# Threshold attention and a token/channel MLP on one core: the second layer of the token MLP taken by halves of the tokens, its second half between later products

## The chip, the core and the metric

The kernel runs on one core of one Trainium2 chip. The metric is the device time of one execution in microseconds (us); five executions were timed and their median is the time given. All arithmetic is float32.

The core has five engines with a queue of instructions each: PE (TensorE, the matrix products, with its weight loads shown apart as PEld), DVE (VectorE), ACT (ScalarE), POOL (GpSimd) and SP (SyncE, which here only issues transfers). Each works through its queue in the order in which the program emitted it, and waits on semaphores for the others. Products are written to PSUM, from where DVE or ACT must take them.

## What is computed

```python
# q, k, v: (8, 8, 576, 64) = (row, head, token, dim)
scores = scale * q @ k.T                              # per row and head
thresh = max(scores, -1) - tau
scores = where(scores >= thresh, scores, -1e9)
attn = exp(scores - max(scores)) ; attn = attn / sum(attn)
x = (attn @ v) as (8, 576, 512)                       # token, model dim
# token MLP, mixes the tokens of a row
h = relu(x.T @ w_tok1) @ w_tok2                       # 576 -> 256 -> 576
u = x + h.T
# channel MLP, mixes the model dim of a token
out = u + relu(u @ w_ch1) @ w_ch2                     # 512 -> 1536 -> 512
```

## The kernel before

**Units.** The attention of the eight rows is cut into 144 units, 18 for each row (`units`, line 84). Row b holds units 18b to 18b+17, and a unit is 128 queries of two heads. The loop at line 614 emits for each unit u, in this order:

1. `scores(u)` (L304): the score products of both heads on PE, then two maxima on DVE (L309) and a bias on POOL (L310).
2. `norm(u-1)`: 1/sum on DVE (L333, L334) and the scaling on POOL (L337).
3. `fill(0.4)`: steps of MLP work, see below.
4. `turn_blocks(u-2)` (L367): a block transpose on DVE. After each third of them sixteen transfers `eT<-T` are issued on SP (L376), which complete the transpose of the attention weights.
5. `weigh(u)`: ACT's two threshold passes (L319), `fill(0.2)`, ACT's first exponential (L326), `fill(0.2)`, its second, `fill(0.2)`.
6. Loads of later q and k on ACT's queue, loads of v on SP's.
7. If a group of three units is due: `values` (L411, L416), the product with v on PE, which reads the tile that the sixteen transfers write. It is due two units after them. ACT copies its result into `xT` (L421).

When the last `values` of row b is done, `push(b)` (L579) puts the MLP work of the row on the queue of steps `todo`.

**The token MLP of a row** (`token_mlp`, L428) is 15 steps: five `turn_x` (L447, transposes on PE, copied by ACT, L448), two `tok1` (L454, ten matmul instructions, relu on ACT, L456), and eight `tok2(c, f)` (L464). `tok2(c, f)` makes, for the quarter c of the model dim and the half f of the tokens (288 each), two products (four matmul instructions) and adds them on DVE to `xT` (L468). The order before is c outside, f inside. For row 0 the first two quarters have been done earlier, at one step a unit (`early`).

**The channel MLP** (`channel_mlp`, L482) works on groups of 256 tokens of a pair of rows, five groups i = 0 to 4, the last of 128. The pair's even row pushes groups 0 and 1, the odd row groups 2, 3 and 4. So group 0 reads tokens 0 to 255 of the even row, and group 2 the last 64 of the even and the first 192 of the odd row. Each group is twelve `ch1(j)` (L507, eight matmul instructions, relu by ACT into `g`, L508), and for each of its two blocks of 128 tokens four `ch2(t, part)` of three products (L528, six matmul instructions of 512 columns). After the last part DVE adds u and writes `us` (L540; L546 in the first pair, where PE adds u by transposes, L524) and SP sends `us` to `out` (L547). From the second pair on, `ch1(1)` is followed by `turn_u` (L491), a DVE transpose of the group's u into the one buffer `us`, which therefore waits for the last `out` transfer of the group before; sixteen SP transfers (L497) then complete u in `ut`.

`tok1`, `tok2`, `ch1` and `ch2` share two PSUM buffers (`ps_mm`); a `ch2` block keeps one of them through all its parts. A product of the next step but one thus waits until DVE or ACT has emptied the buffer.

**The queue of steps.** Each step carries a cost. `push` takes what is left of the queue as `old`, puts one old step ahead of each token MLP step (two ahead of the steps in `waits`, the first `tok1` and the first `tok2`), then the rest of `old`, then the new groups. It sets `quota` = (sum of all costs - KEEP) / 17, KEEP being 45 (20 at row 0). `fill(share)` adds share x quota to the credit and emits steps as long as the credit is above zero, so the last one may overdraw it. Below, a unit's fills are called F.4, and the three F.2.

Of the kernel before, what the change touches and what calls it, by code (L numbers as in the profile page):

```python
# [21 lines left out]
def kernel(  # L22
# [36 lines left out]
    NP = H // 2  # L59
    NTK = DTOK // P  # L60
    NCC = DM // P
    NJ = DCH // P
# [162 lines left out]
    def weight(n):  # L225

        nonlocal steps_done
        for k in range(steps_done, min(steps_done + n, 3 * len(pieces) + 1)):
            i, part = divmod(k, 3)
            if part == 0:  # L230
                on_gpsimd(i - 1)
                if i:
                    load_piece(i - 1 + NRAW)
            else:
                on_scalar(i + 1, part - 1)
            on_vector(i, part)
            steps_done = k + 1
# [5 lines left out]
    def need(i):  # L243

        weight(3 * i + 4 - steps_done)
# [182 lines left out]
    def token_mlp(b, ps=range(NP)):  # L428

        xT = xTs[b]  # L430
        o = S * (b % 2)
        L = len(ps)
        cols = slice(P * ps[0], P * ps[0] + P * L)
        if b not in hidden:
            hidden[b] = work.tile([P, NTK, DM], F32, tag="a", bufs=1, name=f"a_{b}")
        a = hidden[b]

        def psum(name):
            return (ps_mm or ps_tr).tile([P, DM], F32, tag="mm" if ps_mm else "tr", name=name)

        def turn_x(t, n):
            M = MT[t]
            to = ps_tr.tile([P, MAIN], F32, tag="tr", name=f"tx_{b}_{t}_{ps[0]}")[0:M, 0 : n * L * P].rearrange("p (t c x) -> p t c x", t=n, c=L)
            for i in range(n):
                for c in range(L):
                    tok = o + (t + i) * P
                    nc.tensor.transpose(out=to[:, i, c, :], in_=xT[:, ps[c], tok : tok + M], identity=ident)  # L447
            nc.scalar.copy(out=x_sb[0:M, t : t + n, cols], in_=to.rearrange("q t p d -> q t (p d)"))  # L448

        def tok1(m):  # L450
            need(2)
            to = psum(f"t1_{b}_{m}_{ps[0]}")[:, 0 : P * L]
            for t in range(NT):
                nc.tensor.matmul(to, lhsT=w1[:, t, P * m : P * m + P], rhs=x_sb[:, t, cols], start=(t == 0), stop=(t == NT - 1))  # L454
            if ps_mm:
                nc.scalar.activation(out=a[:, m, cols], in_=to, func=AF.Relu)  # L456
            else:
                copies.append(lambda: nc.vector.tensor_scalar(out=a[:, m, cols], in0=to, scalar1=0.0, scalar2=None, op0=ALU.max))

        def tok2(c, f):  # L460
            need(6)
            to = psum(f"t2_{b}_{c}_{f}")[:, 0:HS]
            for m in range(NTK):
                nc.tensor.matmul(  # L464
                    to, lhsT=a[:, m, P * c : P * c + P], rhs=w2[:, m, HS * f : HS * f + HS], start=(m == 0), stop=(m == NTK - 1)
                )
            u = xT[:, c, o + HS * f : o + HS * f + HS]
            nc.vector.tensor_add(out=u, in0=u, in1=to)  # L468

        n = NI // L  # L470
        steps = [(0.11 * n * L, lambda t=t: turn_x(t, n)) for t in range(0, NI, n)] + [(0.11 * L, lambda: turn_x(NI, 1))]
        first = len(steps)
        steps += [(1.1 * L, lambda m=m: tok1(m)) for m in range(NTK)]
        steps += [(0.97, lambda c=c, f=f: tok2(c, f)) for c in ps for f in range(2)]
        return steps, (first, first + NTK)


# [4 lines left out]
    def channel_mlp(b, uT, i):  # L482

        s = {}
        n = min(GR, 2 * S - GR * i)
        nt = n // P

        def turn_u():

            us, ut = s["us"], s["ut"]  # L490
            nc.vector.transpose(  # L491
                out=us[:, 0:nt].rearrange("q n a (c d) -> q c (n a) d", c=NCC),
                in_=uT[:, :, GR * i : GR * i + n].rearrange("q c (m r) -> q c m r", r=32),
            )

            def move(a, k):
                nc.sync.dma_start(out=ut[32 * a : 32 * a + 32, 0:nt, k, :], in_=us[32 * k : 32 * k + 32, 0:nt, a, :])  # L497

            moves.extend([lambda a=a, k=k: move(a, k) for a in range(4) for k in range(4)])

        def ch1(j):
            need(7 + j)
            if j == 0:
                s["g"] = work.tile([P, NJ, GR], F32, tag="g", bufs=1, name=f"g_{b}_{i}")
            ps = ps_mm.tile([P, GR], F32, tag="mm", name=f"c1_{b}_{i}_{j}")[:, 0:n]
            for c in range(NCC):
                nc.tensor.matmul(ps, lhsT=wc1[:, j, c, :], rhs=uT[:, c, GR * i : GR * i + n], start=(c == 0), stop=(c == NCC - 1))  # L507
            nc.scalar.activation(out=s["g"][:, j, 0:n], in_=ps, func=AF.Relu)  # L508
            if j == 1:
                s["us"] = work.tile([P, GR // P, 4, NCC * 32], F32, tag="us", bufs=1, name=f"us_{b}_{i}")  # L510
                if b:
                    s["ut"] = work.tile([P, GR // P, 4, NCC * 32], F32, tag="ut", bufs=1, name=f"ut_{b}_{i}")
                    turn_u()

        def ch2(t, part):
            need(7 + NJ + 3 * part + 2)
            t0 = GR * i + P * t
            if part == 0:
                s["ps"] = ps_mm.tile([P, NCC, P], F32, tag="mm", name=f"c2_{b}_{i}_{t}")
            ps = s["ps"]  # L520
            flat = ps.rearrange("q c d -> q (c d)")
            if part == 0 and not b:
                for c in range(NCC):
                    nc.tensor.matmul(  # L524
                        ps[:, c, :], lhsT=uT[:, c, t0 : t0 + P], rhs=ident, is_transpose=True, start=(c == 0), stop=False, skip_group_check=True
                    )
            for j in range(3 * part, 3 * part + 3):
                nc.tensor.matmul(  # L528
                    flat,
                    lhsT=s["g"][:, j, P * t : P * t + P],  # L530
                    rhs=wc2[:, j, :],
                    start=(j == 0 and b > 0),
                    stop=(j == NJ - 1),
                    skip_group_check=True,
                )
            if part == 3:
                o = s["us"][:, t].rearrange("q a x -> q (a x)")
                if b:
                    move_u()
                    nc.vector.tensor_add(  # L540
                        out=o.rearrange("q (c k d) -> q c k d", c=NCC, k=4),
                        in0=ps.rearrange("q c (k d) -> q c k d", k=4),
                        in1=s["ut"][:, t].rearrange("q k (c d) -> q c k d", c=NCC),
                    )
                else:
                    nc.vector.tensor_copy(out=o, in_=flat)  # L546
                nc.sync.dma_start(out=out[b : b + 2].rearrange("b s d -> (b s) d")[t0 : t0 + P, :], in_=o)  # L547

        return [(0.0067 * n, lambda j=j: ch1(j)) for j in range(NJ)] + [
            (2.6 if part or b else 3.0, lambda t=t, part=part: ch2(t, part)) for t in range(nt) for part in range(4)  # L550
        ]

    def move_u():
        while moves:
            moves.popleft()()
# [6 lines left out]
    todo = deque()  # L562
# [16 lines left out]
    def push(b):  # L579
        nonlocal quota  # L580
        uT = xTs[b]
        steps, waits = token_mlp(b) if b else token_mlp(b, range(NP // 2, NP))
        old = list(todo)
        todo.clear()
        todo.extend(early)
        early.clear()

        for i, step in enumerate(steps):
            n = 2 if i in waits else 1
            todo.extend(old[:n] + [step])  # L590
            del old[:n]
        todo.extend(old)
        for i in range(2) if b % 2 == 0 else range(2, (2 * S + GR - 1) // GR):
            todo.extend(channel_mlp(b - b % 2, uT, i))
        quota = (sum(c for c, _ in todo) - (KEEP if b else KEEP_FIRST)) / (UB - 1)

    prep(0)
# [16 lines left out]
    for u in range(len(units) + LAG + 4):  # L614
# [4 lines left out]
        if on:  # L619
            b_now, p0, t = units[u]  # L620
            n = b_now * NP + p0
# [5 lines left out]
        last = False  # L627
        visit = False
        if due and not in_blocks(due[0][1]):
            visit = due[0][0] <= u  # L630
            last = values_due(u)
# [14 lines left out]
        if last and u < UB:  # L646
            early.extend(token_mlp(0, range(NP // 2))[0])
        elif last:
            push(0)
# [79 lines left out]
```

## Time and profile before

| | |
|---|---|
| median of 5 runs | 1354.51 us (1352.55 to 1356.74) |
| the profiled execution, device time | 1356.74 us |
| its span from first to last instruction | 1355.0 us |
| PE busy | 1307.7 us |
| DVE, ACT, POOL busy | 593.8, 585.2, 352.4 us |
| `tok2` matmuls (L464) | 256 instructions, 75.2 us; idle PE just ahead of them 8.1 us |
| `ch1` (L507), `ch2` (L528) matmuls | 401.4 us, 389.5 us |
| sixteen `eT<-T` transfers of a group, on SP's queue | 10.3 to 13.8 us to issue, median 2.3 us from issue to landing |

A line of the timeline gives the start in us, the length in us, the engine, the line of the kernel, the operation, output<-input, its shape and how many instructions are merged; in brackets the idle time of the engine before it and what ended it. In the list of groups the last columns are busy time, mean ns of one, and idle time before. PEclk is the granted clock of TensorE in tenths.

### The profile page before, as it was taken

The numbers are of one execution on the slowest core, as the hardware profiler recorded it, in microseconds if no ns is written. First come the engines' busy times: TensorE is split into PE (matmuls) and PEld (weight loads), VectorE is DVE, ScalarE is ACT, GpSimd is POOL, SyncE is SP. The second block draws the span as 40 slices with busy tenths as digits, with TensorE's granted clock in tenths as the row PEclk, the third lists the DMA queues.
The fourth block names the chain that finished last, engine by engine and source line by source line (L and its number), as shares of the span: only waits on it lengthen the run. The fifth ranks groups of instructions, "written<-read, shape, count | busy, mean of one in ns | idle before, by whom it ended". The sixth has DMA issues, their size and how long they took to land.

```text
span 1355.0 us, 17794 instructions
## 1 busy us (share of the span) xinstructions
PE 1307.7 (97%) x6138; PEld 810.5 (60%) x6138; DVE 593.8 (44%) x1024; ACT 585.2 (43%) x1299; POOL 352.4 (26%) x683
## 2 busy tenths in 40 slices
PE   6888899999999999999999999999999999999998
PEld 4555556547474666565665566465657566575675
DVE  6878884435443435434334444435443454201000
ACT  6876564444444435443434444344434454120110
POOL 4565652222322222212222222222221222100000
PEclk9998899999999999999999999999999999999999
DMA  5433764535354444543345434534443453400000
GB/s 122 119 94 112 203 157 106 127 93 132 88 133 91 110 107 100 125 110 87 87 105 128 97 85 117 129 81 110 113 101 83 114 117 78 113 22 17 23 24 32
DMA packets 296538, 135.31 MB, mean 100 GB/s; under 512 B 204736, under 2 KB 289216, under 8 KB 296448
## 3 DMA queue, kind: packets, MB, share of 16 engines
q1 hardware_dynamic: 167840, 118.15, 34.2%
q10 hardware_dynamic: 128608, 16.01, 7.4%
q8 instruction: 49, 0.80, 0.2%
q14 instruction: 41, 0.34, 0.1%
HBM read 43.25 MB, written 9.44 MB: 39 GB/s over the span
## 4 chain that ended last, share of the span: by engine, by line
PE 87%; DVE 5%; ACT 3%; DMA 2%; SPq 1%; issue 1%; POOL 1%; ACTq 0%; DVEq 0%; POOLq 0%
PE c L528 27%; PE c L507 27%; PE sc L304 11%; PE pv L416 8%; PE t L454 5%; PE t L464 4%; PE pv L411 3%; DVE mx L309 2%; ACT e L319 1%; PE tx L447 1%; SPq L376 1%; DMA lk<-in_k_dram 1%; PE tr L355 1%; ACT e L326 1%; DMA scratch<-in_moe_w_ch_dram 0%
## 5 line engine op out<-in xcount | busy, mean ns | idle before, releaser
L507 PE MATMUL c<-xT,wc 128*128 128x256 f32 (+1 forms) x1920 | 401.4, 363 | 0.1
L309 DVE TENSOR_REDUCE mx<-sc 128x1 f32<-128x576 f32 x288 | 204.3, 750 | 447.8 <-PE sc L304 447.7
L528 PE MATMUL c<-wc,g 128*128 128x512 f32 x864 | 389.5, 597 | 0.0
L507 PEld LDWEIGHTS c<-xT,wc 128*128 128x128 f32 x1920 | 335.6, 191 | 69.9 <-issue 29.7
L310 POOL TENSOR_SCALAR bias<-mx,toff 128x1 f32<-128x1 f32 x288 | 81.6, 283 | 781.0 <-DVE mx L309 724.2
L319 ACT ACTIVATE e<-sc,bias 128x576 f32<-128x576 f32 x288 | 199.4, 739 | 181.9 <-POOL bias L310 177.9
L528 PEld LDWEIGHTS c<-wc,g 128*128 128x128 f32 x864 | 158.9, 190 | 181.6 <-issue 177.9
L326 ACT ACTIVATE e<-e,ntau 128x576 f32<-128x576 f32 x288 | 221.0, 771 | 0.0
L337 POOL TENSOR_SCALAR e<-e,rr 128x576 f32<-128x576 f32 x288 | 214.4, 756 | 14.7 <-ACT g L508 2.6
L508 ACT ACTIVATE g<-c 128x256 f32<-128x256 f32 (+1 forms) x240 | 86.6, 361 | 297.6 <-PE c L507 279.4
L304 PE MATMUL sc<-kT,qT 64*128 64x288 f32 (+1 forms) x1280 | 194.2, 436 | 13.2 <-DVE kT L286 7.1
L367 DVE STREAM_TRANSPOSE T<-e 128x1152 f32<-128x1152 f32 x126 | 172.0, 1365 | 5.5 <-DMA eT<-T 3.3
L304 PEld LDWEIGHTS sc<-kT,qT 64*128 64x128 f32 (+1 forms) x1280 | 107.6, 180 | 99.9 <-issue 57.7
L416 PE MATMUL pv<-eT,lv 128*64 128x384 f32 (+1 forms) x1024 | 137.1, 408 | 0.0
L416 PEld LDWEIGHTS pv<-eT,lv 128*64 128x64 f32 x1024 | 76.3, 138 | 49.6 <-issue 41.4
L421 ACT COPY xT<-pv 128x384 f32<-128x384 f32 (+1 forms) x56 | 21.0, 400 | 165.6 <-PE pv L416 163.7
L540 DVE TENSOR_TENSOR us<-c,ut 128x512 f32<-128x512 f32 x27 | 18.6, 690 | 155.0 <-PE c L528 137.9
L464 PE MATMUL t<-w,a 128*128 128x288 f32 x256 | 75.2, 421 | 8.1 <-DVE xT L468 4.7
L454 PE MATMUL t<-x_sb,w 128*128 128x512 f32 (+1 forms) x180 | 73.4, 555 | 0.0
L464 PEld LDWEIGHTS t<-w,a 128*128 128x128 f32 x256 | 45.8, 192 | 30.2 <-issue 10.5
L468 DVE TENSOR_TENSOR xT<-xT,t 128x288 f32<-128x288 f32 x64 | 28.3, 446 | 71.0 <-PE t L464 70.5
L326 ACT ACTIVATION_READ_ACCUMULATOR e<-e,ntau 128x1 f32 x288 | 56.6, 197 | 0.0
(46 smaller groups left out, 542.6 us busy)
## 6 DMA issues: line engine op xcount, KB each, us to landing
eT<-T SPq DMA_DIRECT2D x672, 108.0 KB, 2.3
scratch<-in_moe_w_ch_dram SPq DMA_DIRECT2D x24, 512.0 KB, 3.7
lv<-in_v_dram SPq DMA_DIRECT2D x32, 288.0 KB, 3.4
out_dram<-us SPq DMA_DIRECT2D x36, 256.0 KB, 2.2
lk<-in_k_dram ACTq DMA_DIRECT2D x111, 72.0 KB, 2.7
lq<-in_q_dram ACTq DMA_DIRECT2D x106, 72.0 KB, 2.3
ut<-us SPq DMA_DIRECT2D x192, 32.0 KB, 1.9
lq<-in_q_dram SPq DMA_DIRECT2D x22, 72.0 KB, 3.2
```

Of the source, the lines that this page charges most:

```text
L304: nc.tensor.matmul(sc[h][rows, f, 0:HS], lhsT=qT[r, cols], rhs=kT[r, HS * f : HS * f + HS], start=True, stop=True)
L309: nc.vector.tensor_reduce(out=mx[:, c], in_=sc[h][:, :, 0:HS], axis=AX.XY, op=ALU.max)
L319: nc.scalar.activation(out=eh, in_=sc[h][:, :, 0:HS], func=AF.Prelu, bias=bias[:, h : h + 1], scale=SCALE, alpha=STEEP)
L326: nc.scalar.activation(out=eh, in_=eh, func=AF.Exp, bias=ntau, accum_out=rs[:, h : h + 1])
L337: nc.gpsimd.tensor_scalar(out=eh, in0=eh, scalar1=rr[:, h : h + 1], scalar2=1.0, op0=ALU.mult, op1=ALU.mult)
L367: nc.vector.transpose(out=T[:, :, place, :].rearrange("p a (c x) -> p c a x", c=NK), in_=e.rearrange("p (c a x) -> p c a x", c=NK, a=4))
L416: nc.tensor.matmul(to[r], lhsT=lv[:, j, :], rhs=e[j], start=False, stop=(c == NI - 1), skip_group_check=True)
L454: nc.tensor.matmul(to, lhsT=w1[:, t, P * m : P * m + P], rhs=x_sb[:, t, cols], start=(t == 0), stop=(t == NT - 1))
L464: nc.tensor.matmul(to, lhsT=a[:, m, P * c : P * c + P], rhs=w2[:, m, HS * f : HS * f + HS], start=(m == 0), stop=(m == NTK - 1))
L507: nc.tensor.matmul(ps, lhsT=wc1[:, j, c, :], rhs=uT[:, c, GR * i : GR * i + n], start=(c == 0), stop=(c == NCC - 1))
L508: nc.scalar.activation(out=s["g"][:, j, 0:n], in_=ps, func=AF.Relu)
L528: nc.tensor.matmul(flat, lhsT=s["g"][:, j, P * t : P * t + P], rhs=wc2[:, j, :], start=(j == 0 and b > 0), stop=(j == NJ - 1), skip_group_ ...
```

## The change

`tok2` now runs through all four quarters c for the first half of the tokens, then for the second half. `push` takes the second half (four steps, two for row 0) off the token MLP and puts them between the first `ch1` steps of the row's first new group: `ch1(0)`, `tok2`, `ch1(1)`, `tok2`, and so on. With eleven token steps instead of fifteen, fewer old steps are used up among them. At `waits` row 1 takes three old steps at both places, rows 2, 4 and 6 three ahead of the first `tok2`, the others two as before. In group 1 of the first pair (`b == 0 and i == 1`), which is the old work of row 1, a `ch2` step holds one product instead of three (J = 1).

```diff
-        steps += [(0.97, lambda c=c, f=f: tok2(c, f)) for c in ps for f in range(2)]
+        steps += [(0.97, lambda c=c, f=f: tok2(c, f)) for f in range(2) for c in ps]
...
+        J = 1 if b == 0 and i == 1 else 3
...
-        def ch2(t, part):
-            need(7 + NJ + 3 * part + 2)
+        def ch2(t, part, J):
+            need(7 + NJ + J * part + J - 1)
...
-            for j in range(3 * part, 3 * part + 3):
+            for j in range(J * part, J * part + J):
...
-            if part == 3:
+            if J * part + J == NJ:
...
-            (2.6 if part or b else 3.0, lambda t=t, part=part: ch2(t, part)) for t in range(nt) for part in range(4)
+            (0.867 * J + (0.0 if part or b else 0.4), lambda t=t, part=part: ch2(t, part, J)) for t in range(nt) for part in range(NJ // J)
...
         steps, waits = token_mlp(b) if b else token_mlp(b, range(NP // 2, NP))
+        half = NP if b else NP // 2
+        last = steps[-half:]
+        del steps[-half:]
...
         for i, step in enumerate(steps):
-            n = 2 if i in waits else 1
+            n = (3 if b == 1 or (b % 2 == 0 and i == waits[1]) else 2) if i in waits else 1
             todo.extend(old[:n] + [step])
             del old[:n]
         todo.extend(old)
+        new = []
         for i in range(2) if b % 2 == 0 else range(2, (2 * S + GR - 1) // GR):
-            todo.extend(channel_mlp(b - b % 2, uT, i))
+            new.extend(channel_mlp(b - b % 2, uT, i))
+        for i, step in enumerate(last):
+            new.insert(2 * i + 1, step)
+        todo.extend(new)
```

## The prediction, made before the changed kernel was run

> **What bounds the kernel now.** I read the page's busy times and slices first, then the list of groups, then PE's timeline from end to end for its gaps, and last SP's timeline beside it.
>
> ```profile
> PE 1307.7 (97%) x6138; PEld 810.5 (60%) x6138; DVE 593.8 (44%) x1024; ACT 585.2 (43%) x1299; POOL 352.4 (26%) x683
> ...
> PE   6888899999999999999999999999999999999998
> ...
> L464 PE MATMUL t<-w,a 128*128 128x288 f32 x256 | 75.2, 421 | 8.1 <-DVE xT L468 4.7
> ```
>
> PE sets the end. Its work isn't touched: the same instructions run, in another order. Only its gaps can change: 1355.0 - 1307.7 = 47.3 us, of which some 26 lie ahead of 133 us, where hardly anything is moved, and 3.9 at the very end. That leaves about 17. The groups put 8.1 of them ahead of tok2. One by one, in PE's timeline:
>
> ```profile
> 140.09 2.29 PE L464 MATMUL t<-w,a 128*128 128x288 f32 x4 [2.91 <-DVE xT L468]
> 161.82 1.87 PE L304 MATMUL sc<-kT,qT 64*128 64x288 f32 x8 [2.57 <-ACT e L319]
> 163.63 7.08 PE L507 MATMUL c<-xT,wc 128*128 128x256 f32 x24
> ...
> 250.33 0.55 PE L411 MATMUL pv<-eT,vl 128*64 128x192 f32 x4 [2.46 <-DMA lk<-in_k_dram]
> 285.79 0.63 PE L447 MATMUL tx<-ident,xT 128*64 128x128 f32 x4 [1.23 <-ACT x_sb L448]
> 304.31 1.24 PE L464 MATMUL t<-w,a 128*128 128x288 f32 x4 [1.26 <-DVE xT L468]
> 309.38 3.23 PE L464 MATMUL t<-w,a 128*128 128x288 f32 x12 [0.52 <-DVE xT L468]
> 433.16 0.87 PE L411 MATMUL pv<-eT,vl 128*64 128x384 f32 x4 [0.34 <-ACT e L326]
> 458.70 1.24 PE L464 MATMUL t<-w,a 128*128 128x288 f32 x4 [1.58 <-ACT g L508]
> 774.03 1.24 PE L464 MATMUL t<-w,a 128*128 128x288 f32 x4 [0.82 <-ACT g L508]
> 830.88 1.90 PE L304 MATMUL sc<-kT,qT 64*128 64x288 f32 x8 [0.78 <-ACT e L319]
> ```
>
> The waits for tok2 are short ones for a PSUM buffer. The second bound is less plain: the wait at 250.33 is named a load, but it ends 2.56 us after SP has issued the group's sixteen eT transfers (234.57 + 13.20 = 247.77). `values` waits for those, and in rows 1 and 2 they are hardly ever early. The same comparison two units on from 366.76, where unit 52 starts:
>
> ```profile
> 371.08 13.41 SPq L376 DMA_DIRECT2D eT<-T  x16
> ...
> 387.23 0.55 PE L411 MATMUL pv<-eT,vl 128*64 128x192 f32 x4
> ```
>
> Issue ends at 384.49, the last lands some 2.2 later (1.9 to 2.6 where PE waited for it) at 386.7, and PE arrives at 387.23: 0.5 us to spare. So the question is which steps stand between a group's sixteen transfers and its `values`.
>
> **How the order was worked out.** I carried costs, quota and credit through the units for both orders. Row 1, for instance: quota before (129.4 - 45)/17 = 4.97, after (130.3 - 45)/17 = 5.02, so a unit gets 1.99 in F.4 and 0.99 in each F.2. The order before agrees with the trace (unit 43 gets tok2 in each F.2: 300.85 x8, 304.31 x4). Durations used: scores 1.17 (start to next start), ch1 1.79 (x24 takes 5.38), a ch2 step of three 2.67, tok2 0.97 to 1.07.
>
> **Part 1, tok2 by halves.** Nothing is added on any engine or queue; 28 + 2 steps move later, behind 1 to 4 of the new ch1. ch1(0) now follows the adds of the first half more closely.
> - Row 0, unit 22. Before: tok2, tok2, [2.91], tok2, ch1(0). After: tok2, ch1(0), whose last quarter needs that add. The add sits on DVE behind the maxima of unit 22 as before (139.59), so PE has 1.5 us of ch1 to run from 136.05 and then waits 2.6. The wait at 161.82 follows a weight load that SP issues behind the sixteen transfers of this unit; with one add (0.45) less ahead of the transpose these start 0.4 earlier. **Gain 0.4** (bounds -1.0 and +2.9).
> - Row 1: the third tok2 of unit 43 still finds both buffers full (1.26 stays). In unit 44 ch1(0) waits some 0.3 for the last add instead of 0.52. **Gain 0.2.**
> - Row 2, unit 63: three small ch1 instead of two ahead of tok2. The third waits 0.9 for its buffer, tok2 0.3 more, but 0.98 of work more is done: 1.58 + 0.98 - 1.2 - 0.9. **Gain 0.5** (0 to 1.6). Rows 4 and 6: the third ch1 meets the same wait that tok2 met. **0.** In F.4 two tok2 with one small ch1 between them show a gap of 0.24 (782.87 starts 1.13 after 781.74 where 0.89 is usual); by the new order row 4 loses one such place and row 6 gets two. **Loss 0.3.**
> - Rows 3, 5, 7 show no gap before. After, the half moved stands between ch1 of 1.79, and each add ends some 3.5 us into its unit (maxima 1.42, norm 0.35, add 0.45 behind scores 1.17), PE needing the buffer at 4.0. **0**; without that cover it would be 0.4 a row.
>
> **Part 2, older work.** Before, 5.2 cost is left when row 1 is pushed, two steps; after, 6.07, seven single products (the first group's two boundaries fall otherwise). They go between the five turn_x, and the 0.24 and 1.23 idle ahead of them go: ACT needs 0.57 for each copy, a product covers 0.87. **Gain 1.3** of 1.47. None is left for the first tok1's third place, nor for tok2: the "three" of row 1 does nothing. A switch between products of two tiles shows up to 0.10 in the lengths (2.84 against 2.74), seven of them at most 0.7; I take 0, as most rows after a turn_x read 2.74.
>
> **Part 3, what the shift does to `values`.** In each window I compared work before and after, and when the transfers start. Most have over 1 us to spare. The tight ones:
> - Unit 36 (250.33): single products overdraw less, two instead of three ahead of it. **Loss 0.9**, the gap becomes 3.3.
> - Unit 54 (387.23): one ch2 step (the second of group 2's second block) slips from unit 52 into 51, and nothing comes in its place; 2.67 less in the window against 0.5 to spare. **Loss 2.2** (0.5 to 2.7). Unit 51 gets the 2.67, where there was no gap to fill.
> - Unit 60 (433.16): 2.67 more. **Gain 0.3.**
> - Units 69 and 105. The last ch2 of the old group, with its output, slips from behind the sixteen transfers to ahead of them (unit 67 and 103, F.4). The transpose now waits for that product and add: 1.17 + 2.6 + 0.69 against 3.05 after the unit's start, 1.5 later, and 0.35 for the out transfer on SP. `values` had 0.1 and 0.7 to spare, with +0.5 and -0.3 of work. The load on ACT's queue that lengthened the issue (13.80 and 12.41, against 10.30 undisturbed) is then partly past. **Loss 0.6 and 1.0** (0 to 2.0 each).
>
> The same slip ends a worse thing on DVE:
>
> ```profile
> 492.89 13.80 SPq L376 DMA_DIRECT2D eT<-T  x16
> 506.80 0.53 SPq L547 DMA_DIRECT2D out_dram<-us  x1
> ...
> 509.10 1.25 DVE L491 STREAM_TRANSPOSE us<-xT 128x1024 f32<-128x1024 f32 x1 [8.00 <-DMA out_dram<-us]
> 827.80 1.25 DVE L491 STREAM_TRANSPOSE us<-xT 128x1024 f32<-128x1024 f32 x1 [10.01 <-DMA out_dram<-us]
> ```
>
> turn_u held DVE for 8.00, 10.01 and (row 6) 3.31 us until the output behind the transfers had gone. PE paid only once, at 830.88: 0.78 idle and scores of 1.90 instead of 1.24. **Gain 1.4.**
>
> **Sum.** Gains 0.4 + 0.2 + 0.5 + 1.3 + 0.3 + 1.4 = 4.1; losses 0.3 + 0.9 + 2.2 + 1.6 = 5.0. Net +0.9. The profiled execution took 1356.74, 1.74 more than its span and 2.2 more than the median, so it would take 1357.6; the median goes from 1354.5 to **1355.4**.
>
> A rule is to be weighed here. The gap of 2.57 at 161.82 cost clock (twelve products in 7.08 instead of 5.45, scores 1.87 for 1.24; granted clock 0.63 from 164 to 168 us), the gap of 2.46 at 250.33 none (1.00). So from the rows alone a gap of 3.3 or 2.2 may cost nothing, or 0.63 + 1.63 + 0.62 = 2.9; I take 0, the nearest row in place. The Trainium skill (TensorE: Matmul & The Clock Gate, Part 1: The HAM clock gate) says the clock halves after an idle window of about 3.4 us that runs freely; the two rows show that 2.5 can already do it and need not. By the page a full cold window at unit 36 would cost some 1.7 us, an estimate, making the sum 1357.1.
>
> **Rivals.**
> 1. *Faster: the transfers keep up.* For it: landing times run from 2.2 to 4.3 us and issue from 10.3 to 13.8, and a shift of ACT's loads out of the issue alone would save 3 us at units 54, 69 and 105. Against: ACT's loads follow the units and still fall inside. Then the losses of 3.8 there (2.2 + 1.6) go: 1355.4 - 3.8 = 1351.6; if the tok2 waits go wholly as well (2.6 + 1.3 + 0.3 + 1.1 + 1.6 = 6.9) 1344.7. I put it at 1350.
> 2. *Slower: the longer gaps cool the clock*, at unit 36, at 54, or both: 1355.4 + 2.9 = 1358.3, or 1361.2. It decides from the point where a gap loses clock, which the rows only place near 2.5.
> 3. *Slower: turn_u blocks the moved adds.* The second tok2 of the half moved is behind turn_u on DVE. If the output still stands behind the sixteen transfers, DVE is held 8.0, 10.0 and 3.3 us; PE gets through tok2, ch1 and scores (4 us), then stands: 4 + 6 = 10 more, 1365. By the queue arithmetic the output comes in F.4, ahead of them; one step later and it doesn't.
> 4. *Part 2 doesn't do what it says*, if the single products all go ahead of the token steps: 1355.4 + 1.3 = 1356.7; no other sign than the forecast's.
>
> **How the numbers follow.** This kernel's measurement can tell about 0.2% (2.7 us) from no change: 1351.8 to 1357.2. Forecast with rival 4: 0.44, its own range 1351.8 to 1357.2 (its bounded terms add to about 2.5 either way). Rival 1: 0.26. Rival 2: 0.21. Rival 3: 0.09. Faster 0.26, the same 0.44, slower 0.30. The range reaches into rivals 1 and 2, to 1350.0 and 1360.5, leaving out the far end of rival 1 and rival 3.
>
> **What would show it.** PE's gaps: none ahead of turn_x near 285; 1.26 still ahead of a tok2 in unit 43; about 3.3 ahead of the `values` of unit 36, 2 ahead of that of unit 54, about 1 ahead of those of 69 and 105; L491 without its waits of 8 and 10, and no 0.78 near 831. Wrong would be a wait of DVE at L491 followed by one of PE at L464, a granted clock under 0.9 behind unit 36 or 54, or no gap at `values` of 54.

## The result, and the profile after

| | before | after |
|---|---|---|
| median | 1354.5 us (1350.66 to 1358.75, 51 runs) | 1357.53 us (1354.11 to 1362.27, 29 runs) |
| ratio to before, 95% interval | | 1.0025 [1.0019, 1.0031] |
| the profiled execution, and its span | 1356.74, 1355.0 us | 1360.33, 1358.5 us |

The changed kernel is 3.0 us slower, 2.1 us above the forecast, inside the range. 0.25% is just past what was called no change.

The page of the changed kernel: engines' busy time, the granted clock in 40 slices, and two groups of the list.

```profile
PE 1310.7 (96%) x6138; PEld 812.8 (60%) x6138; DVE 592.1 (44%) x1024; ACT 584.0 (43%) x1299; POOL 352.7 (26%) x683
...
PEclk9998999999999999999999999999999999999999
...
L464 PE MATMUL t<-w,a 128*128 128x288 f32 x256 | 76.3, 422 | 1.4 <-DVE xT L468 1.3
L411 PE MATMUL pv<-eT,vl 128*64 128x384 f32 (+1 forms) x256 | 46.7, 433 | 9.1 <-DMA lq<-in_q_dram 4.5
```

The change did to tok2 what it says: idle PE ahead of L464 falls from 8.1 to 1.4 us. Idle time ahead of `values` (L411) rises to 9.1 (5.2 in the list of before), and ahead of ch1 (L510) to 6.1 (0.1 at L507 before). PE's timeline, the gaps that matter:

```profile
142.06 1.22 PE L510 MATMUL c<-xT,wc 128*128 128x256 f32 x2 [2.59 <-DVE xT L468]
162.82 1.86 PE L304 MATMUL sc<-kT,qT 64*128 64x288 f32 x8 [1.58 <-ACT e L319]
...
250.60 0.65 PE L411 MATMUL pv<-eT,vl 128*64 128x192 f32 x4 [2.71 <-DMA lq<-in_q_dram]
305.25 1.24 PE L464 MATMUL t<-w,a 128*128 128x288 f32 x4 [1.26 <-DVE xT L468]
319.29 1.99 PE L510 MATMUL c<-xT,wc 128*128 128x256 f32 x8 [0.55 <-DVE xT L468]
390.07 0.55 PE L411 MATMUL pv<-eT,vl 128*64 128x192 f32 x4 [1.49 <-DMA eT<-T]
...
536.92 0.55 PE L411 MATMUL pv<-eT,vl 128*64 128x192 f32 x4 [1.25 <-DMA lk<-in_k_dram]
854.08 0.55 PE L411 MATMUL pv<-eT,vl 128*64 128x192 f32 x4 [1.26 <-DMA lq<-in_q_dram]
```

Nothing is left ahead of turn_x near 285, nor at 831. New are `values` of units 54 (390.07), 72 (536.92) and 108 (854.08), and a ch1 in unit 46 (319.29). The gap of unit 36 (250.60) is only 0.25 longer than before, but it now costs clock. The windows view has stretch, length, busy time of each engine (instructions), granted clock, DMA share and GB/s:

```profile
251.00:254.00 3.00, 3.00 (x22) 2.86 (x20) 0.00 (x0) 0.00 (x0) 0.00 (x0) 0.50 0.30 56
```

TensorE ran at half clock there. The same stretch of before, by its own gap of unit 36:

```profile
250.00:252.00 2.00, 1.67 (x21) 1.70 (x23) 0.00 (x0) 0.00 (x0) 0.00 (x0) 1.00 0.50 112
252.00:255.00 3.00, 3.00 (x32) 2.24 (x27) 0.00 (x0) 0.54 (x2) 0.00 (x0) 1.00 0.00 0
```

To add up what no single gap shows, I took for each matmul the time from its start to the next one's start, less the usual one for its kind and shape in before. This excess by stretch (us from the start), for before, after and runs that are told of below:

```
               before  after |    e1     e5     e6     e8     e9
 131 to 172     12.83  10.65 | 10.74   9.63  16.10  10.02  10.50
 172 to 230      3.54   4.61 |  5.82   4.06   3.02   4.95   8.45
 230 to 260      3.73   5.70 |  3.06   3.79   1.47   3.11   1.51
 260 to 300      3.45   1.50 |  3.41   4.80   1.51   3.03   1.48
 300 to 345      3.91   4.59 |  4.39   3.16   3.14   3.14   3.23
 380 to 415      1.69   2.83 |  1.59   1.47   1.40   3.03   1.39
 485 to 530      2.14   1.68 | 10.09   1.66   1.65   1.73   1.49
 530 to 580      1.88   3.02 |  1.82   1.83   2.61   1.73   1.83
 800 to 830      2.06   1.10 |  3.24   2.68   1.04   2.47   1.24
 830 to 885      2.66   3.58 |  2.00   2.02   2.05   2.05   2.05
1070 to 1120     3.17   4.38 |  3.90   3.43   3.69   3.83   3.68
all from 131    65.22  66.96 | 74.67  61.59  59.91  62.48  59.10
```

The sums move by some tenths of a us, up to 0.7 in a stretch, with what is taken as usual, so only the larger differences are read. In this pair of profiles the change is worth +1.7 us. The other 1.9 us of the two spans' difference of 3.5 lie ahead of 131 us, before anything is moved.

### The profile page after: what moved, and what is told of

Read it like the earlier page. It is cut to its first block, busy times and chain, and to the rows that moved or that the text cites. A ratio compares the mean times of both kernels' runs of the same rounds, so it can differ in the third digit from the quotient of the medians.

```text
span 1358.5 us, 17797 instructions
## 1 busy us (share of the span) xinstructions
PE 1310.7 (96%) x6138; PEld 812.8 (60%) x6138; DVE 592.1 (44%) x1024; ACT 584.0 (43%) x1299; POOL 352.7 (26%) x683
## 4 chain that ended last, share of the span: by engine, by line
PE 85%; DVE 6%; DMA 3%; ACT 2%; issue 1%; POOL 1%; SPq 0%; ACTq 0%; DVEq 0%; POOLq 0%
PE c L532 27%; PE c L510 25%; PE sc L304 11%; PE pv L416 9%; PE t L454 5%; PE t L464 4%; PE pv L411 3%; DVE mx L309 2%; DMA lq<-in_q_dram 1%; PE tx L447 1%; ACT e L319 1%; DMA lk<-in_k_dram 1%; PE tr L355 1%; DVE scratch L203 1%; ACT e L326 1%
## 5 line engine op out<-in xcount | busy, mean ns | idle before, releaser
L510 PE MATMUL c<-xT,wc 128*128 128x256 f32 (+1 forms) x1920 | 402.3, 361 | 6.1 <-DVE xT L468 3.3
L510 PEld LDWEIGHTS c<-xT,wc 128*128 128x128 f32 x1920 | 333.7, 190 | 73.8 <-issue 24.2
L464 PE MATMUL t<-w,a 128*128 128x288 f32 x256 | 76.3, 422 | 1.4 <-DVE xT L468 1.3
L464 PEld LDWEIGHTS t<-w,a 128*128 128x128 f32 x256 | 46.4, 192 | 22.2 <-issue 10.6
L411 PE MATMUL pv<-eT,vl 128*64 128x384 f32 (+1 forms) x256 | 46.7, 433 | 9.1 <-DMA lq<-in_q_dram 4.5
```

The source lines that it names most:

```text
L411: nc.tensor.matmul(to[r], lhsT=vl[:, r], rhs=e[NI], start=True, stop=False, skip_group_check=True)
L464: nc.tensor.matmul(to, lhsT=a[:, m, P * c : P * c + P], rhs=w2[:, m, HS * f : HS * f + HS], start=(m == 0), stop=(m == NTK - 1))
```

## The experiments

Ratios are to runs of before on the same chip in the same set; its medians there were 1356.08 (e1 to e4), 1353.66 (e5 to e8) and 1355.6 us (e9 to e12).

**e1, the halves alone.** After, but with ch2 steps of three products and two older steps at the waits everywhere:

```diff
-        J = 1 if b == 0 and i == 1 else 3
+        J = 3
...
-            n = (3 if b == 1 or (b % 2 == 0 and i == waits[1]) else 2) if i in waits else 1
+            n = 2 if i in waits else 1
```

> tok2 by halves and its second half between the ch1, but steps of three products in all groups and two older steps at both waits, as before. Theory (the single products are the loss: they leave 0.87 us of cost more or less in a unit, which moves a whole ch2 step over a unit's boundary in later rows): no gap of its own ahead of the values of units 36, 54 and 72, idle gaps there as in the kernel before (2.5, 0, 0 us); the wait of 8 us of DVE at turn_u in row 2 may stay, the gaps ahead of turn_x (1.6) stay; row 0 some 1 us better. Time 0 to 2 us below before. Rival (the halves are the loss: ch1 and tok2 wait for the adds, and the adds stand behind turn_u): 2 to 3 us above before, with gaps at tok2 and ch1.

1367.27 us, 1.0088 [1.0074, 1.0102], against all that was expected. The timeline shows one place; rows of SP, DVE and PE:

```profile
492.40 13.36 SPq L376 DMA_DIRECT2D eT<-T  x16
505.87 1.10 SPq L551 DMA_DIRECT2D out_dram<-us  x1
...
508.63 1.25 DVE L494 STREAM_TRANSPOSE us<-xT 128x1024 f32<-128x1024 f32 x1 [9.00 <-DMA out_dram<-us]
...
511.53 3.78 PE L510 MATMUL c<-xT,wc 128*128 128x256 f32 x8 [6.05 <-DVE xT L468]
```

The last output of the old group stands on SP behind the sixteen eT transfers. turn_u, which overwrites `us`, waits on DVE for it until 508.63. The moved tok2's add (L468) is queued behind turn_u and ends at 511.5, and the ch1 that needs the add's PSUM buffer leaves PE idle for 6.05 us. The granted clock is 0.56 from 509 to 513 us and 0.58 from 513 to 517. This is the third rival of the prediction, and it costs 8 us of excess (10.09 against about 2) in this one unit.

**e2, the single products alone.** Before with J = 1 in group 1 of the first pair; tok2 in its old order and place.

> Steps of a single product in the older work of row 1, nothing else: tok2 in the old order, all of it ahead of ch1, two older steps at both waits. Theory (the single products are the loss): the gaps ahead of turn_x are gone (1.6 to 1.9 us gained), and gaps appear ahead of the values of unit 54 (1.5 to 2.2 us) and unit 72 (1.4), the gap of unit 36 is 0.3 to 0.9 longer, with a window of half clock after it in some executions (1.7): 1.5 to 3 us above before. Rival (the halves are the loss): 1 to 2 us below before, since only the gaps at turn_x change.

1357.59 us, 1.0009 [0.9999, 1.002], between the two expectations and not clear of no change. The turn_x gaps go, as they should (excess of 260 to 300: 1.50), but `values` of unit 54 waits 1.31 and unit 36's gap of 2.43 is followed by half clock from 252.08 on. The gap foreseen at unit 72 isn't there. What one place gains, two others lose.

**e3 and e4, the third older step.** e3 is after with J = 3 (halves and threes), e4 is after with n = 2 at all waits (halves and singles).

> The change with steps of three products in all groups, the three older steps at the waits kept. Theory: like the run with the halves alone, within 1 us, so 0 to 2 us below before; row 1 has only two older steps for its fifteen places, so three or two makes nothing there, and in rows 2, 4 and 6 the wait of 0.8 to 1.7 us moves from tok2 to a ch1. Rival (the halves or the third older step are the loss): 2 to 3 us above before.

> The change with two older steps at both waits everywhere, single products and halves kept. Theory: as the changed kernel within 1 us, 2 to 4 us above before; the gaps at the values of units 36, 54 and 72 stay. Rival (the third older step is the loss): at or below before.

e3: 1366.8 us, 1.0083 [1.0069, 1.0096], with e1's stall: the threes don't remove it. e4: 1360.58 us, 1.0027 [1.0014, 1.004], like after (1.0025). The third older step is worth nothing that can be measured. So it is the single products that take the stall away from the halves: they leave 0.87 more cost in the queue, and the old group's last output slips ahead of the sixteen transfers. After's SP queue shows it, 1.3 us between the two:

```profile
496.47 0.36 SPq L551 DMA_DIRECT2D out_dram<-us  x1
497.80 10.96 SPq L376 DMA_DIRECT2D eT<-T  x16
508.87 14.13 SPq L500 DMA_DIRECT2D ut<-us  x16
523.12 10.95 SPq L376 DMA_DIRECT2D eT<-T  x16
```

The last two rows are the source of unit 72's gap: the sixteen ut transfers come right behind the eT transfers and take 14.13 us to issue; the next sixteen eT start at 523.12, though their block transposes were done at 520.2. In before the ut transfers start later, behind a pause of the queue, and take less time:

```profile
510.37 10.19 SPq L497 DMA_DIRECT2D ut<-us  x16
```

Two loads go out on ACT's queue during either set (512.73 and 513.09 after, 512.89 and 515.44 before); the last section comes back to that.

**e5, the stall's cause taken away.** e1, with turn_u issued at the eighth ch1 of a group instead of the second, when all moved adds are ahead of it:

```diff
-            if j == 1:
+            if j == 7:
                 s["us"] = work.tile(
```

> The halves of the tokens alone (steps of three and two older steps at the waits, as before), but the transpose turn_u is issued with the eighth ch1 of a group instead of the second, behind all moved tok2 steps. Theory (turn_u, which waits on VectorE for the out transfer behind sixteen eT transfers, holds up the moved adds; that alone makes the halves 11 us slower): the 6.05 us gap in unit 67 and the 6.8 us of half clock behind it go, the excess of 485 to 530 falls from 10.1 to about 2, and the time is 0.999 to 1.002 of before. Rival (the moved half itself costs, by its place between the ch1 steps): the gap comes back at another unit and the ratio stays above 1.005.

1354.65 us, 1.0002 [0.9992, 1.0012], and 1.66 of excess from 485 to 530. One number changed, and 0.86% is gone (8.4 us of it in this stretch by the two profiles): the blocked DVE queue is what made the halves slow. Halves without single products, with turn_u later, are then worth nothing measurable; what the later turn_u alone does to before wasn't run.

**e6, later `values`.** After, with the `values` of rows 1 to 7 emitted behind the next unit's scores:

```diff
         elif early:
             early.popleft()[1]()
+        if due and in_blocks(due[0][1]):
+            values_due(u - 1)
         if 0 < u <= len(units):
...
-        if due and in_blocks(due[0][1]):
-            values_due(u)
```

> The kernel after, with values for rows 1 to 7 issued behind the next unit's scores instead of ahead of them, 1.17 us of products later. Theory (what is left of the loss is values waiting for the last of the sixteen eT transfers): the gaps ahead of L411 in units 36, 54, 72, 96 and 108 (2.71, 1.49, 1.25, 0.49, 1.26) lose up to 1.17 each, 5.2 in all, the half clock after unit 36 goes with them, 1.7: some 7 below after, 0.996 to 0.999 of before. Rival (the gap only moves to the scores or to their exponentials, because PE has no less to do before the transfers land): the ratio stays at 1.001 to 1.003.

1351.11 us, 0.9982 [0.9973, 0.999]: 0.43%, 5.8 us, below after's 1.0025 (two sets of runs). Ahead of `values` only 0.87 in unit 72 is left above 0.3 us behind 131 us, and excess in 230 to 260 falls from 5.70 to 1.47. Not foreseen was unit 25:

```profile
160.75 2.92 PE L304 MATMUL sc<-kT,qT 64*128 64x288 f32 x8 [4.93 <-ACT e L319]
```

There ACT is behind because it waits for the channel weights (5 transfers issued from 153.03, ACT starts on them at 156.51 after 3.88 us idle), and the `values` just moved away was PE's work meanwhile. Half clock for 6.83 us follows.

**e7, the same edit on before.**

> The kernel before with the same edit as in the run with values issued later. Theory: before has one such gap (unit 36, 2.46) and small ones, so it gains 1 to 2, ratio 0.998 to 0.9995, and the two kernels then differ by 4 to 5 us less than 7 in favour of neither: after with the edit is within 0.1% of before with it or faster. Rival (the later values cost something of their own): ratio 1.000 to 1.003.

1359.46 us, 1.0037 [1.0024, 1.0049], the wrong sign. Unit 25 stalls here too (5.44). Row 4 adds a stall that before hides; DVE and PE in its timeline:

```profile
823.33 1.25 DVE L491 STREAM_TRANSPOSE us<-xT 128x1024 f32<-128x1024 f32 x1 [9.15 <-DMA out_dram<-us]
...
826.40 1.93 PE L304 MATMUL sc<-kT,qT 64*128 64x288 f32 x8 [3.31 <-ACT e L319]
```

This is the 0.78 us of before at 830.88, without the `values` that stood ahead of those scores and covered most of it. It is turn_u's wait again, which the change removes and this edit doesn't. So with this edit on both, the change is 8.4 us faster (1351.11 against 1359.46 in the same set); some 5 of that are this stall and the one window of half clock behind it (828.14 to 831.55).

**e8, turn_u later in after.** After with e5's edit.

> The kernel after, with turn_u issued with the eighth ch1 instead of the second. Theory (the ut transfers, now right behind the last eT group, meet the loads on ACT's queue, take 14.1 and 14.5 instead of 10.2, and delay the eT transfers of units 70 and 106, so that units 72 and 108 wait 1.25 each): these two gaps go and the ratio falls from 1.0025 by 0.001 to 0.002. Rival (those transfers are late whatever stands before them): units 72 and 108 still wait over 0.8 and the ratio stays at 1.002 to 1.004.

1356.8 us, 1.0025 [1.0012, 1.0038]. The trace does what the theory says, the time doesn't. The ut transfers go behind the next sixteen eT and take 10.43 us, and the gaps of units 72 and 108 are gone:

```profile
528.75 10.43 SPq L500 DMA_DIRECT2D ut<-us  x16
```

1.3 and 1.5 us of excess go with them (530 to 580, 830 to 885), but 1.4 comes back in 800 to 830, where `values` of unit 105 now waits 0.60. So the ut transfers ahead of the eT transfers are shown as the source of the two gaps, while the time that their removal is worth isn't shown: the interval still holds the low end of what was expected, 0.1%.

**e9, `values` later from unit 27 on.** e6, with row 1's first `values`, due in unit 24, left where it was (`u > 26` added to the new condition, and the old call kept for `u < 26`).

> As the run of after with values issued later, but the values of unit 24 stay ahead of the scores of unit 25, where ScalarE is held up by the channel weights' loads and 3.4 us of values were what TensorE had to do meanwhile. Theory: the gap of 4.93 us in unit 25 falls back to about 1.7 and the stretch of half clock behind it from 6.83 to 3.41 us or none: 3.2 + 1.7 to 3.4 us less than with all values later, ratio 0.993 to 0.996. Rival (the 0.9982 was due to the drift of other waits, and the exchange is worth nothing there): 0.997 to 0.999.

1351.39 us, 0.9963 [0.9948, 0.9977], between the two ranges expected and the lowest ratio of all, 4 to 5 us below before and, by the ratios of two sets, some 8 below after. The intervals of e6 and e9 touch, so the better of the two isn't settled. Unit 25 is back to 1.57; the same stall then turns up three units on, where row 1's second `values` is the first one moved:

```profile
161.68 1.86 PE L304 MATMUL sc<-kT,qT 64*128 64x288 f32 x8 [1.57 <-ACT e L319]
...
187.10 2.44 PE L304 MATMUL sc<-kT,qT 64*128 64x288 f32 x8 [2.84 <-ACT e L319]
```

ACT again starts late on a channel weight (5.47 us idle before 184.76). Excess of 172 to 230 is 8.45 against 3.02 in e6. A start still later, at unit 30, wasn't tried.

**e10, e11, e12: what the change is worth once its waits are gone.** All three have turn_u at the eighth ch1 and `values` later from unit 27; e10 on the halves alone, e11 on after, e12 on before.

> The halves alone (steps of three, two older steps at the waits) with turn_u at the eighth ch1 and values behind the scores from unit 27. Theory: the gain of later values (some 4) on top of the halves with the late turn_u (1.0002): 0.995 to 0.998, above the same with single products by their gain ahead of turn_x, 1.5 to 2 us. Rival (single products cost as much elsewhere as they save at turn_x): within 0.5 us of it.

> The kernel after with turn_u at the eighth ch1 and values behind the scores from unit 27. Theory: all waits that the change brought are gone, and its gains at turn_x, in row 0 and in row 2 stay: 0.993 to 0.996, and 2.5 to 4.5 us below the kernel before with the same two edits. Rival (the change as such is worth nothing once these waits are gone from both): within 1 us of it.

> The kernel before with turn_u at the eighth ch1 and values behind the scores from unit 27: what the two edits are worth without the change. Theory: the gap of unit 36 (2.5) goes, the 1.9 at turn_x, the 1.3 and 0.5 at the tok2 of row 1 and the 1.0 of row 0's second half-clock stretch stay: 0.996 to 0.999. Rival: as fast as the kernel after with the same edits, 0.993 to 0.996.

| | median | ratio to before |
|---|---|---|
| e10, halves | 1355.16 us | 0.9994 [0.9984, 1.0004] |
| e11, halves, singles, threes | 1352.97 us | 0.9978 [0.9965, 0.9991] |
| e12, none of the change | 1354.5 us | 0.9983 [0.9973, 0.9994] |

The two edits are worth 0.17% to before as well, as expected. e10 and e11 are slower than their ranges: all three keep the stall of unit 28 (2.71, 2.77 and 2.88 us, with half clock behind it), and in e11 `values` of unit 105 still waits 0.72. e11 is 1.5 us below e12: the gain of 2.5 to 4.5 that was expected isn't there. Whether any is left isn't settled: with the runs of both resampled, their medians differ by -0.2 to 2.9 us (95%). e10 is 2.2 above e11 (0.9 to 3.6 in the same way), as expected from the 1.24 us gap at turn_x that it keeps (excess of 260 to 300: 3.39 against 1.63). e9, the change with `values` later alone, is 3.1 below e12 (1.3 to 5.9) in the same set; before with e9's edit alone, which would be its partner, wasn't run.

## Why the prediction was nearly right, and where it wasn't

By its own steps, in the excess of the two profiles or in gaps:

- **Sum.** Forecast +0.9, profiles +1.7, medians +3.0. The terms were right in kind, several of them wrong by 1 to 2 us in size or place. That the sum came near is partly luck: row 0 gained more than forecast and units 69 and 105 lost nothing, against what was lost at units 36, 72 and 108.
- **Forecast or rival 2.** The median of 1357.53 is 0.8 below rival 2's 1358.3 and 2.1 above the forecast, and that rival's sign came: a granted clock of 0.50 behind unit 36.
- **"Only its gaps can change."** From the scores at 134.15 us (136.13 after) to the end, PE's idle time rises from 20.9 to 21.2 us and its busy time from 1199.9 to 1201.2. Waits inside a record and half clock count as busy, so the gaps alone couldn't give the sum.
- **Row 0, gain 0.4.** 2.2 came in 131 to 172: the gaps fell from 2.91 to 2.59 and from 2.57 to 1.58, and the second no longer cost clock, for which the 0.4 had nothing. That before paid clock there is luck of the clock's phase (last section).
- **turn_x, gain 1.3.** 1.95 of excess; the two gaps of 0.24 and 1.23 are gone. Singles do it alone (e2). Right.
- **Unit 63, gain 0.5.** 0.6 (445 to 485: 3.25 to 2.67). Right. **Unit 60, gain 0.3.** Right: its gap of 0.34 is gone. The loss of 0.3 in rows 4 and 6 wasn't looked for.
- **turn_u in row 4, gain 1.4.** 1.0 in 800 to 830; L494 doesn't wait there. Right in mechanism.
- **Unit 44, gain 0.2.** The 0.52 went, but ch1 waits 0.55 in unit 46 and 0.19 in unit 44: 300 to 345 lost 0.7. The step said that in rows 3, 5 and 7 the adds are out of the way in time and was applied to row 1 only for its first unit. The moved half's adds go on for two more, and in unit 46 ch1 (319.29) waits for the add of the tok2 just ahead of it, which DVE, idle for 0.53 us by then, starts at 318.78 as soon as that product has ended.
- **Unit 54, loss 2.2.** 1.1, the gap 1.49. Right place, half the size, inside its bounds.
- **Units 69 and 105, loss 1.6.** None there. The transfers behind the output took 10.96 and 11.30 us, not 13.8 and 12.4, which made up for their later start. The loss came one group later, at 72 and 108 (1.1 and 0.9). The slip of the output was worked out for the sixteen eT transfers that follow it, and not for the sixteen ut transfers, which it moved forward (510.37 to 508.87, 829.08 to 826.29) and which then took 14.13 and 14.49 us in place of 10.19. e8, where they go later, shows them as the cause.
- **Unit 36, loss 0.9 and no clock.** This is the step that failed most. The gap grew by 0.25, to 2.71 instead of the 3.3 forecast, and the clock fell: +2.0. "I take 0, the nearest row in place" was the wrong choice, and the price of rival 2, 2.9, was wrong too. Its 0.63 and 0.62 fit scores of 1.87 (161.82) and 1.86 (170.65) in place of 1.24; after runs scores in 1.86 at a granted clock of 1.00 (162.82), so that is a wait inside the record and no clock. What is left, 1.63 for the twelve products, is near the 1.7 that a stretch of 3.41 us at half clock costs. The Trainium skill's figure (TensorE: Matmul & The Clock Gate, Part 1: The HAM clock gate), 1.7 as an estimate, was the better price.
- **Part 2's "three", nothing.** e4 agrees.
- **Not predicted and not taken apart:** 1.1 in 172 to 230 and 1.2 in 1070 to 1120. In the second it isn't the wait of `values`, which is shorter than before (0.22 at 1071.20 after, 0.32 at 1068.46 before).
- **Rival 3.** Priced at 10 us, and in place and sign just what e1 has (+11 us), one step away: "by the queue arithmetic the output comes in F.4, ahead of them; one step later and it doesn't". e1 and e3 are that one step. The arithmetic was right, and it decided more than all the other terms together.

Where did the gain go, then? Of the 6.7 us of idle that left tok2, most was only passed on to ch1 (idle ahead of L510 is 6.1 us in the list of after, ahead of L507 0.1 before), and what the single products gained at turn_x was lost again where `values` waits for transfers that start no earlier. With most of those waits gone from both kernels (e11, e12), 1.5 us are left, and they aren't clear of noise.

## What to carry to other kernels

Before moving a step, ask what it will stand behind on its engine's queue: an add behind a transpose that waits for an output transfer made the halves 11 us slower, 8 of them counted at that place, and issuing that transpose six steps later took it away. Where a product waits for transfers, more work ahead of it is worth more than filling gaps elsewhere (e6 and e9, 0.2% and 0.4% below before, on a change that lost 0.25%); but look at each place that gives work away, since in units 25 and 28 that work covered something else, and on before the same edit lost 0.37% (e7). Test a part both alone and with the others: halves alone cost 11 us, singles alone about 1, together 3.

## What the runs showed of the hardware

**The clock falls on a fixed grid.** In all fourteen profiles the stretches of half clock start at whole multiples of 3.413 us from each other: after, for instance, has them at 100.73, 114.38, 141.69 and 250.92, that is 0, 4, 12 and 44 steps. The grid starts anywhere with respect to the kernel. Cutting PE's timeline by each profile's own grid tells which gaps cost clock. For the gap of unit 36:

```
            gap, us   of it in one step of the grid   next step at half clock
before       2.46                1.44                          no
e1           1.66                1.52                          no
e8           1.84                1.84                          no
e3           2.43                1.50                          no
e5           2.52                1.98                          no
e4           2.36                2.17                          yes
e2           2.43                2.32                          yes
after        2.71                2.71                          yes
```

Two gaps of 2.43 differ only in where the grid cut them. Over all steps at full clock from 120 to 1200 us, the 19 with 2.0 us idle or more were all followed by half clock, none with up to 1.64 was, and between these it went both ways (no at 1.98, yes at 1.67). Behind a step that was idle throughout (e1, e6, e7), half clock lasted two steps, in e6 with only 0.19 us idle in the first of them. The Trainium skill (TensorE: Matmul & The Clock Gate, Part 1: The HAM clock gate) states a free-running window of 3413 ns, and the grid agrees; it asks for an idle window, and these runs show that 2.0 of 3.41 us idle are enough. So a gap of 2.4 to 2.7 us, such as those of units 22 and 36, is followed by a window of half clock, 1.7 us, in some profiles and not in others. As each kernel was profiled once, how much of the spread of 8 us between executions of before comes from this isn't shown. No gap under 1.6 us cost clock.

**Loads on ACT's queue hold up the issue on SP's.** In the fourteen profiles, from 230 us on, 178 sets of sixteen eT or ut transfers were issued with no load on ACT's queue meanwhile and took 10.1 to 11.6 us; 564 sets with one load or more took 10.2 to 17.0, with a median of 12.0. The extra time goes by in one or two pauses: in the set of 14.13 us (after, 508.87) the transfers follow each other every 0.64 us, and once only after 4.61, around the two loads of 512.73 and 513.09. It isn't always SP that pauses: in the set of 10.19 us (before, 510.37) two loads went out as well, SP kept its pace, and the second load came 2.55 us after the first instead of 0.36. What decides between the two isn't shown.
